# A gated mix of sliding-window attention and an MLP, one decode step: order and shape of the first and last transfers

## The chip, the cores and the metric

The kernel runs on one core of one Trainium2 chip. The metric is the device time of one launch in microseconds (us). The engines are named as in the profile: PE (TensorE matmul), PEld (its weight loads), DVE (VectorE), ACT (ScalarE), POOL (GpSimd) and SP (SyncE, which here only issues transfers). A "q" behind a name is the engine's sequencer. Sixteen DMA engines move the data.

## The reference

One token `x` of 576 elements goes through two branches, which a scalar gate mixes. All inputs are bf16.

```python
def reference(A_x, A_k_cache, A_v_cache, A_wq, A_wo, B_x, B_w1, B_b1, B_w2, B_b2, gate_w):
    x = A_x                                               # [1, 1, 576]
    g = sigmoid((x * gate_w).sum(-1, keepdims=True))
    # attention: 32 query heads, 16 KV heads of width 128, the last 4096 of 32768 keys
    q = (x @ A_wq).reshape(1, 1, 32, 128).transpose(0, 2, 1, 3)
    k = repeat(A_k_cache[:, :, -4096:, :], 2, axis=1)
    v = repeat(A_v_cache[:, :, -4096:, :], 2, axis=1)
    p = softmax(einsum("bhqd,bhkd->bhqk", q, k) * 128 ** -0.5)
    o = einsum("bhqk,bhkd->bhqd", p, v)
    a = o.transpose(0, 2, 1, 3).reshape(1, 1, 4096) @ A_wo
    # MLP: 576 -> 4608 -> 576
    h = gelu_tanh(x @ B_w1 + B_b1)
    b = h @ B_w2 + B_b2
    return g * a + (1 - g) * b                            # [1, 1, 576]
```

Keys and values are 16.8 MB each, the four weight matrices 4.7 or 5.3 MB each: some 53.6 MB are read once for an output of 1,152 bytes.

## The kernel before, in words

**Loads.** Nearly every load is issued by SP on one queue. A load of keys or values (`load_kv`, L102) brings two heads: for each head 64 partitions, each with one row of 16,384 bytes. The first 64 partitions of the tile are the first head, the others the second. Eight such loads bring the keys, eight the values, into a pool of six tiles, which w_2 shares at the end. The matrices w_q, w_1 and w_o go through a pool of three tiles; `load_flat` (L120) brings a slice of the matrix that is laid out flat over 128 partitions, so that each partition gets one contiguous row: 18,432 bytes for each of the two w_q tiles.

**Order of the issues.** The schedule is written by hand: the program text is the order on each engine. SP's order at the start is k_t[0] (L102), x9 (L136, x spread over 64 partitions, 9 elements each), the two w_q tiles (L120), k_t[1] and k_t[2] (L102), then the halves of b_1 (L557), w_1 and further keys and values. Three rows of 576 elements are issued by ACT instead: x_row (L130), gw_row (L131, the gate's weights) and b_2 into row 0 of b2_r (L132). POOL clears b2_r first (L129), so the load of b_2 waits for that clearing, while those of x_row and gw_row wait for nothing. The framework hands each transfer one of eight completion counters in turn; a transfer that gets a counter again waits for the counter's last user to have landed.

**Start of the computation.** PE first spreads x9 over the partitions (x_ps, L373), from which DVE makes the columns x2 (L381). DVE multiplies x_row and gw_row and sums them (L385), PE spreads the sum (g_ps, L390), and ACT and DVE make the gate g and omg = 1 - g of it (L392 to L397). Behind g_ps on PE stand the transposes of the first two heads' keys (L235), the product with w_q (q_ps, L409: 36 matmuls, of which the first four read the first 2,048 elements of the first tile), its turning (L421), and the first scores (L266).

**The middle.** For each head its keys are turned by PE (L235) and evicted by ACT and DVE (L246, L244). Scores (L266), softmax, and values (L342) follow behind. The two halves of w_1 are multiplied between the heads.

**The end.** The attention's output times w_o and the first three groups of w_2 are summed on PE in `part` (L671), with four rows of `part` on four column groups of the array at once. w_2 comes in four groups of nine rows per partition; the third is loaded in two pieces (rows 0 to 4, 5 to 8), the fourth in three (rows 0 to 5, 6 and 7, 8), all at L629. DVE adds (1 - g) times b_2 to `part` (part_s, L679). Then `row_matmul` (L690) sums the partitions of part_s and adds the nine rows of the last w_2 group into y_ps: output quarter t of 144 columns stands on partition 32 t. So the last four matmuls use row 8, one quarter each. DVE evicts all of y_ps with one instruction (L703), and SP writes the four partitions 0, 32, 64 and 96 of y to the output (L704).

In the profile trailing digits are left out of names: b_r is b2_r or b1_r, w_t is w1_t or w2_t, x is x9 or x2.

Of the kernel before, what the change touches and what calls it, by code (L numbers as in the profile page):

```python
# [9 lines left out]
BF16 = mybir.dt.bfloat16  # L10
# [6 lines left out]
def kernel(  # L17
# [15 lines left out]
    nc = tc.nc  # L33

    P = 128
    D = 576
# [10 lines left out]
    NQ = 4  # L47
    DQ = D // NQ

    RJ = 9  # L50
    NG = F // (P * RJ)


    NM = 9


    QC = Hq * Dh // 8
# [21 lines left out]
    const = ctx.enter_context(tc.tile_pool(name="const", bufs=1))  # L79
# [11 lines left out]
    wq_flat = A_wq.rearrange("a b -> (a b)").rearrange("(p n) -> p n", p=P)  # L91
    w1_flat = B_w1.rearrange("a b -> (a b)").rearrange("(p n) -> p n", p=P)
    w2_view = B_w2.rearrange("(g p j) n -> g p (j n)", p=P, j=RJ)
# [5 lines left out]
    def load_kv(cache, m, name):  # L99
        t = kv_pool.tile([P, NCK, Dh], BF16, name=name, tag="kv")  # L100

        nc.sync.dma_start(  # L102
            out=t[:],
            in_=cache[0, 2 * m : 2 * m + 2, Sk - W : Sk, :].rearrange(
                "e (p c) d -> p e (c d)", c=NCK
            ),
        )
        return t

    def load_k(m):  # L110
        return load_kv(A_k_cache, m, "k_t")
# [3 lines left out]

    WMAX = 41 * 256

    def load_flat(src, lo, n, name):
        t = w_pool.tile([P, WMAX], BF16, name=name, tag="w")
        nc.sync.dma_start(out=t[:, 0:n], in_=src[:, lo : lo + n])  # L120
        return t

    k_tiles, v_tiles = {}, {}

    x_row = const.tile([1, D], BF16, name="x_row")
    gw_row = const.tile([1, D], BF16, name="gw_row")

    b2_r = const.tile([P, D], BF16, name="b2_r")
    nc.gpsimd.memset(b2_r[:], 0.0)  # L129
    nc.scalar.dma_start(out=x_row[:], in_=A_x.rearrange("a b d -> (a b) d"))  # L130
    nc.scalar.dma_start(out=gw_row[:], in_=gate_w.rearrange("(o n) -> o n", o=1))  # L131
    nc.scalar.dma_start(out=b2_r[0:1, :], in_=B_b2.rearrange("(o n) -> o n", o=1))  # L132

    k_tiles[0] = load_k(0)
    x9 = const.tile([P // 2, NM], BF16, name="x9")
    nc.sync.dma_start(out=x9[:], in_=A_x.rearrange("a b (i m) -> (a b i) m", m=NM))  # L136
    wq_t = []
    QP = 2 * NM
    for i in range(2):
        wq_t.append(load_flat(wq_flat, i * QP * QC, QP * QC, "wq_t"))  # L140

    k_tiles[1] = load_k(1)

# [12 lines left out]
        out=row_f[:], in_=ident_f[:, 0 : 32 * (NQ - 1) + 1 : 32], axis=AX.X, op=ALU.add  # L156
# [4 lines left out]
        out=dup[:].rearrange("k (i e) -> k i e", e=2),  # L161
        in_=ident[0 : P // 2, 0 : P // 2].rearrange("k (i e) -> k i e", e=1).to_broadcast(
            [P // 2, P // 2, 2]
        ),
    )
    par = const.tile([P, 2], FP32, name="par")
    for o in range(2):
        nc.vector.tensor_reduce(
            out=par[:, o : o + 1],
            in_=ident_f[:].rearrange("p (i o) -> p o i", o=2)[:, o, :],  # L170
# [7 lines left out]
        out=turn[:].rearrange("p j (h q) -> p j h q", h=OJ),  # L178
        in_=ident[:].rearrange("p (o q j) -> p j o q", o=1, j=OJ).to_broadcast(
            [P, OJ, OJ, P // OJ]  # L180
        ),
# [4 lines left out]
        out=m_r[:], in_=ident_f[:].rearrange("p (s r) -> p r s", r=R), axis=AX.X, op=ALU.add  # L186
# [5 lines left out]
        out=row_e[:], in_=ident_f[:].rearrange("p (a e q) -> p e a q", e=2, q=2), axis=AX.XY,  # L192
# [3 lines left out]
        out=row_e[:], in0=row_e[:], scalar1=-MASK, scalar2=MASK, op0=ALU.mult, op1=ALU.add  # L196
    )
    mask = const.tile([P, BC * P], BF16, name="mask")
    for e in range(2):
        nc.vector.tensor_copy(  # L200
            out=mask[:, e::2], in_=row_e[:, e : e + 1].to_broadcast([P, BC * P // 2])
# [4 lines left out]
        out=m_c[:], in_=ident_f[:].rearrange("p (t c r) -> p c t r", c=BC, r=R), axis=AX.XY,  # L206
# [4 lines left out]
        out=m_hl[:], in_=ident_f[:].rearrange("p (h q) -> p h q", h=OJ), axis=AX.X, op=ALU.add  # L211
# [10 lines left out]
    for dst, src in ((sel, ident), (sel_f, ident_f)):  # L222
        nc.vector.tensor_copy(
            out=dst[:].rearrange("p l (o h) -> p l o h", o=2),
            in_=src[:].rearrange("p (h l x) -> p l x h", h=2, l=2)[:, :, 0:2, :],
# [149 lines left out]
    for dst, src, s in (  # L375
# [10 lines left out]
        out=junk[:], in0=x_row[:], in1=gw_row[:], scale=1.0, scalar=0.0,  # L386
# [11 lines left out]
        out=omg[:], in0=g_t[:], scalar1=-1.0, scalar2=1.0, op0=ALU.mult, op1=ALU.add  # L398
# [7 lines left out]
    for b in range(NM * NQ):  # L406
        m, t = b // NQ, b % NQ
# [22 lines left out]
    for m in range(HB // 2):  # L430
        lo = R * (NGR - 1) + RP * m
        nc.vector.tensor_copy(  # L432
            out=qz[:, m :: HB // 2, lo : lo + RP],
            in_=qT[:, :, m, :].rearrange("p i b -> p b i"),
# [7 lines left out]
    def w1_load(i):  # L442
        return load_flat(w1_flat, i * W1N, W1N, "w1_t")
# [105 lines left out]
    for h in range(NU):  # L549
# [4 lines left out]
        if h == 1:  # L554

            for o in range(2):
                nc.sync.dma_start(  # L557
                    out=b1_r[o : o + 32 * (NQ - 1) + 1 : 32],
                    in_=B_b1.rearrange("(o t k n) -> o t k n", o=2, t=NQ, k=2)[o],
# [57 lines left out]
    for i in range(NOG // 2):  # L617
        t = w_pool.tile([P, WMAX], BF16, name="wo_t", tag="w")
        nc.sync.dma_start(
            out=t[:, 0 : 2 * OJ * D].rearrange("p (o n) -> p o n", o=2),  # L620
            in_=wo_view[:, 2 * i : 2 * i + 2, :],
# [2 lines left out]
    w2_t = []  # L624
    for g in range(NG):
        t = kv_pool.tile([P, NCK * Dh], BF16, name="w2_t", tag="kv")
        cut = {NG - 2: (0, 5, RJ), NG - 1: (0, 6, 8, RJ)}.get(g, (0, RJ))
        for lo, hi in zip(cut, cut[1:]):
            nc.sync.dma_start(out=t[:, lo * D : hi * D], in_=w2_view[g, :, lo * D : hi * D])  # L629
        w2_t.append(t)  # L630

    ot = const.tile([P, Hq], BF16, name="ot")
# [1 line left out]
        out=ot[:], in0=o_sb[:], scalar=g_t[:, 0:1], in1=r_sums[:], op0=ALU.mult, op1=ALU.mult  # L634
# [3 lines left out]
    for j in range(OJ):  # L638
# [3 lines left out]
        out=ow_m[:],  # L642
# [5 lines left out]
    with nc.allow_low_precision("one of the eight summands is not zero"):  # L648
        nc.vector.tensor_reduce(  # L649
            out=ow[:].rearrange("p j o -> p (j o)"), in_=ow_m[:], axis=AX.X, op=ALU.add  # L650
# [4 lines left out]
    y_ps = ps_s.tile([P, DQ], FP32, name="y_ps", tag="s")  # L655
# [12 lines left out]
    for n, four in enumerate(blocks):  # L668
# [11 lines left out]
        out=part_s[:], in0=b2_r[:].rearrange("p (k n) -> p k n", k=2), scalar=omg[:, 0:1],  # L680
# [5 lines left out]
    quarters = [slice(t * DQ, (t + 1) * DQ) for t in range(NQ)]  # L686
# [10 lines left out]
    for j in range(RJ):  # L697
# [1 line left out]
        row_matmul(  # L699
            gt[:, j, NG - 1 : NG], [row[:, q] for q in quarters], False, j == RJ - 1  # L700
        )
    y = const.tile([P, DQ], BF16, name="y")
    nc.vector.tensor_copy(out=y[:], in_=y_ps[:])  # L703
    nc.sync.dma_start(  # L704
        out=out.rearrange("a b (t n) -> (a b t) n", t=NQ), in_=y[0 : 32 * (NQ - 1) + 1 : 32, :]
    )


# [28 lines left out]
```

## Time and profile before

| | before |
|---|---|
| time, median of 3 runs (all) | 134.98 us (134.93 to 135.19) |
| profiled execution: time | 134.92 us |
| profiled execution: span, first to last instruction | 133.0 us |
| busy PE / DVE / ACT / POOL | 90.9 / 61.3 / 48.5 / 4.2 us |
| read from memory | 53.62 MB, 403 GB/s over the span |
| first issue on SP (k_t[0]) and on ACT (x_row) | both at 0.73 us |
| POOL's clearing of b2_r | 0.73 us, 0.58 us long |
| x_ps on PE (needs x9) | 8.80 us |
| product of x_row and gw_row on DVE (L385) | 9.61 us |
| first transposes on PE | 10.98 us |
| last group of w_2: start of the first and the last matmul | 128.55 and 129.6 us |
| eviction of y_ps, issue of the result | 129.95 and 130.29 us |

The span counts from the first to the last instruction that the profiler saw; the time of an execution is longer by what lies around it. Windows give, for a stretch of the span, the busy time of each engine, the granted clock of TensorE as a share of its full speed, the mean busy share of the 16 DMA engines, and the rate at which bytes moved. In short windows the last two are rough: a packet's whole length and all of its bytes are booked where it starts.

### The profile page before, as it was taken

What the parts mean: (1) busy time and instruction counts of PE and PEld (TensorE: products, weight loads), DVE (VectorE), ACT (ScalarE), POOL (GpSimd) and SP (SyncE); (2) the same over time, 40 slices, a digit from 0 to 9 for tenths busy, and PEclk for the clock granted to TensorE, in tenths of its full rate; (3) what the DMA queues carried; (4) which work ended last, traced back from release to release, by engine and by line L of the source; (5) the groups of instructions that cost most, each with busy time, mean ns of one, the idle gap of its engine ahead of it and who ended that gap; (6) DMA issues with size and microseconds to landing.
All of it is one profiled execution on the core that took longest, in us unless ns stands there. A gap on an engine that the chain in (4) does not pass through costs nothing.

```text
span 133.0 us, 2659 instructions
## 1 busy us (share of the span) xinstructions
PE 90.9 (68%) x1127; PEld 58.6 (44%) x1127; DVE 61.3 (46%) x165; ACT 48.5 (36%) x91; POOL 4.2 (3%) x11
## 2 busy tenths in 40 slices
PE   0007985299296899969076996978988648459660
PEld 0007741267174565645045654645655215135340
DVE  4964632035227665575004257564866463440020
ACT  3003750066336787757001153766584100000000
POOL 8400000000000000000000000000000000000000
PEclk9999999757999999999955559999999955555865
DMA  3999999999999999999899999999999999999960
GB/s 79 400 430 432 443 424 429 434 436 412 431 458 399 453 414 446 409 421 479 379 453 409 448 414 443 419 439 424 434 429 429 415 418 430 436 424 415 428 261 0
DMA packets 4553, 53.79 MB, mean 404 GB/s; under 512 B 563, under 2 KB 702, under 8 KB 1214
## 3 DMA queue, kind: packets, MB, share of 16 engines
q1 hardware_dynamic: 4536, 53.62, 95.2%
q8 instruction: 9, 0.15, 0.4%
q14 instruction: 2, 0.02, 0.0%
q10 hardware_dynamic: 6, 0.00, 0.0%
HBM read 53.62 MB, written 0.00 MB: 403 GB/s over the span
## 4 chain that ended last, share of the span: by engine, by line
DMA 58%; PE 28%; DVE 8%; SPq 2%; issue 2%; DVEq 0%
DMA w_t<-in_B_w_dram 41%; DMA k_t<-in_A_k_cache_dram 17%; PE tp L235 13%; PE s_ps L266 4%; PE acc L342 3%; DVE kT L244 3%; PE h_ps L454 2%; PE hT L481 2%; DVE a_s L358 2%; PE y_ps L690 1%; SPq L120 1%; SPq L102 1%; DVE ez L320 1%; DVE part_s L679 1%; DVE h_r L472 1%
## 5 line engine op out<-in xcount | busy, mean ns | idle before, releaser
L246 ACT CAST kT<-tp 128x512 bf16<-128x512 f32 x80 | 44.1, 586 | 44.2 <-PE tp L235 43.7
L244 DVE CAST kT<-tp 128x512 bf16<-128x512 f32 x48 | 33.0, 690 | 38.6 <-PE tp L235 34.1
L235 PE MATMUL tp<-ident,k_t 128*128 128x128 bf16 x512 | 45.5, 238 | 4.7 <-DMA k_t<-in_A_k_cache_dram 3.0
L235 PEld LDWEIGHTS <-k_t 128*128 128x128 bf16 x512 | 35.2, 107 | 17.4 <-issue 12.8
L342 PE MATMUL acc<-v_t,ez 128*32 128x512 bf16 x128 | 13.3, 459 | 2.2 <-DVE a_s L358 1.9
L266 PE MATMUL s_ps<-kT,qz 128*32 128x512 bf16 x128 | 13.5, 416 | 0.3 <-DVE qz L432 0.3
L454 PE MATMUL h_ps<-w_t,x 128*32 128x288 bf16 x72 | 4.0, 365 | 6.8 <-DMA w_t<-in_B_w_dram 6.8
L454 PEld LDWEIGHTS <-x 128*32 128x32 bf16 x72 | 2.8, 117 | 7.6 <-issue 7.1
L373 PE MATMUL x_ps<-x,dup 64*128 64x9 bf16 x1 | 0.2, 163 | 8.8 <-DMA x<-in_A_x_dram 8.8
L342 PEld LDWEIGHTS <-ez 128*32 128x32 bf16 x128 | 3.7, 102 | 5.5 <-issue 3.1
L266 PEld LDWEIGHTS <-qz 128*32 128x32 bf16 x128 | 3.3, 94 | 3.8 <-issue 0.8
L679 DVE SCALAR_TENSOR_TENSOR part_s<-b_r,omg,part 128x576 f32<-128x576 bf16 x1 | 0.8, 814 | 8.8 <-PE part L671 8.8
L671 PE MATMUL part<-wo_t,ow 128*1 128x288 bf16 x64 | 4.0, 443 | 1.0 <-DVE ow L649 1.0
L671 PE MATMUL part<-w_t,gt 128*1 128x288 bf16 x54 | 3.7, 364 | 1.4 <-DMA w_t<-in_B_w_dram 1.4
L358 DVE SCALAR_TENSOR_TENSOR a_s<-acc,m_c,a_s 128x128 f32<-128x128 f32 x12 | 4.2, 351 | 0.4
L307 ACT ACTIVATE pr<-ms,nb 128x512 bf16<-128x512 f32 x4 | 2.9, 722 | 4.1 <-DVE nb L304 4.1
L320 DVE COPY ez<-pT 128x64 bf16<-128x64 bf16 x32 | 3.6, 183 | 1.7 <-PE pT L315 1.5
L148 DVE CAST ident_f<-ident 128x128 f32<-128x128 bf16 x1 | 3.0, 3000 | 1.8 <-POOL ident masks.py:199 1.8
L365 PE MATMUL o_ps<-m_r,a_s 128*128 128x8 f32 x8 | 1.9, 315 | 2.8 <-DVE a_s L358 2.8
L365 PEld LDWEIGHTS o_ps<-m_r,a_s 128*128 128x128 f32 x8 | 1.6, 249 | 4.9 <-DVE a_s L358 2.5
L671 PEld LDWEIGHTS <-gt 128*1 128x1 bf16 x54 | 2.2, 104 | 2.9 <-issue 2.0
L481 PE MATMUL hT<-sel_f,h_r 128*64 128x4 f32 x36 | 2.7, 264 | 1.2 <-DVE h_r L472 1.2
(82 smaller groups left out, 48.2 us busy)
## 6 DMA issues: line engine op xcount, KB each, us to landing
k_t<-in_A_k_cache_dram SPq DMA_DIRECT2D x8, 2048.0 KB, 27.5
v_t<-in_A_v_cache_dram SPq DMA_DIRECT2D x8, 2048.0 KB, 24.5
w_t<-in_B_w_dram SPq DMA_DIRECT2D x2, 2592.0 KB
wq_t<-in_A_wq_dram SPq DMA_DIRECT2D x2, 2304.0 KB, 14.4
wo_t<-in_A_wo_dram SPq DMA_DIRECT2D x2, 2304.0 KB
w_t<-in_B_w_dram SPq DMA_DIRECT2D x2, 1296.0 KB, 21.6
w_t<-in_B_w_dram SPq DMA_DIRECT2D x1, 864.0 KB
w_t<-in_B_w_dram SPq DMA_DIRECT2D x1, 720.0 KB, 21.3
```

The source lines that it names most:

```text
L148: nc.vector.tensor_copy(out=ident_f[:], in_=ident[:])
L235: nc.tensor.matmul(tp[:, c * P : (c + 1) * P], lhsT=k_tiles[h // 2][:, (h % 2) * NCH + i * BC + c, :], rhs=ident[:], start=True, stop=True,)
L244: nc.vector.tensor_copy(out=dst, in_=tp[:])
L246: nc.scalar.copy(out=dst, in_=tp[:])
L266: nc.tensor.matmul(s_tiles[b][32 * t : 32 * (t + 1), :], lhsT=qz[:, h // 2, lo : lo + 32], rhs=kT[h][:, i * BC * P : (i + 1) * BC * P], st ...
L320: nc.vector.tensor_copy(out=ez[:, b % 2, m, NQ * s : NQ * (s + 1), :, RP * m : RP * (m + 1)], in_=pT[:].rearrange("p c (t s r) -> p t c s ...
L342: nc.tensor.matmul(acc[b][32 * ct : 32 * ct + 4 * R, :, :], lhsT=ez[:, b % 2, ul // 2, n, :, :].rearrange("p c r -> p (c r)"), rhs=v_tiles ...
L358: nc.vector.scalar_tensor_tensor(out=a_s[:], in0=acc[b][:, c, :], scalar=m_c[:, c : c + 1], in1=a_s[:], op0=ALU.mult, op1=ALU.add,)
L365: nc.tensor.matmul(o_ps[:], lhsT=a_s[:], rhs=m_r[:], start=True, stop=True)
L454: nc.tensor.matmul(h_box[0][32 * t : 32 * (t + 1), k, 0:FB], lhsT=x2[:, m, :], rhs=w[:, off : off + FB], start=(m == 0), stop=(m == NM - 1),)
L481: nc.tensor.matmul(box[0][64 * e : 64 * (e + 1), j, :], lhsT=rows[:, j : j + RJ * 63 + 1 : RJ], rhs=sel_f[:, e, :], start=True, stop=True,)
L671: nc.tensor.matmul(part[32 * t : 32 * t + 1, k, 0:DB], lhsT=col, rhs=w[:, i * D + k * DB : i * D + (k + 1) * DB], start=(n == 0), stop=(n ...
```

## The change

Five places change.

1. `load_flat` can load its tile in pieces, and call a function between the first piece and the second. The first w_q tile is loaded in two: its first 2,048 elements per partition (128 rows of 4,096 bytes, 512 KB) are the first transfer of SP; then come k_t[0] and x9, and then the other 7,168 elements.
2. ACT's first transfers are now those of b_2, which wait for the clearing of b2_r; those of x_row and gw_row come behind them.
3. b_2 and x_row are loaded in halves of 288 elements each.
4. The last row of the last w_2 group is loaded in two pieces: its first 432 elements per partition, and its last 144, which only the last matmul reads.
5. y is a single row of 576 elements on one partition. The four quarters of y_ps are copied into it one by one, t = 0 and 1 by ACT, t = 2 and 3 by DVE. The result is written from one row instead of four.

```diff
-    def load_flat(src, lo, n, name):
+    def load_flat(src, lo, n, name, cuts=(), between=None):
         t = w_pool.tile([P, WMAX], BF16, name=name, tag="w")
-        nc.sync.dma_start(out=t[:, 0:n], in_=src[:, lo : lo + n])
+        edges = (0, *cuts, n)
+        for i, (a, b) in enumerate(zip(edges, edges[1:])):
+            if i == 1 and between is not None:
+                between()
+            nc.sync.dma_start(out=t[:, a:b], in_=src[:, lo + a : lo + b])
         return t
...
     nc.gpsimd.memset(b2_r[:], 0.0)
-    nc.scalar.dma_start(out=x_row[:], in_=A_x.rearrange("a b d -> (a b) d"))
+
+    for o in (slice(0, D // 2), slice(D // 2, D)):
+        nc.scalar.dma_start(out=b2_r[0:1, o], in_=B_b2.rearrange("(o n) -> o n", o=1)[:, o])
+    for o in (slice(0, D // 2), slice(D // 2, D)):
+        nc.scalar.dma_start(out=x_row[:, o], in_=A_x.rearrange("a b d -> (a b) d")[:, o])
     nc.scalar.dma_start(out=gw_row[:], in_=gate_w.rearrange("(o n) -> o n", o=1))
-    nc.scalar.dma_start(out=b2_r[0:1, :], in_=B_b2.rearrange("(o n) -> o n", o=1))
-
-    k_tiles[0] = load_k(0)
+
     x9 = const.tile([P // 2, NM], BF16, name="x9")
-    nc.sync.dma_start(out=x9[:], in_=A_x.rearrange("a b (i m) -> (a b i) m", m=NM))
-    wq_t = []
+
+    def first_keys():
+        k_tiles[0] = load_k(0)
+        nc.sync.dma_start(out=x9[:], in_=A_x.rearrange("a b (i m) -> (a b i) m", m=NM))
...
     QP = 2 * NM
-    for i in range(2):
-        wq_t.append(load_flat(wq_flat, i * QP * QC, QP * QC, "wq_t"))
+    wq_t = [
+        load_flat(wq_flat, 0, QP * QC, "wq_t", (NQ * QC,), first_keys),
+        load_flat(wq_flat, QP * QC, QP * QC, "wq_t"),
+    ]
...
-        cut = {NG - 2: (0, 5, RJ), NG - 1: (0, 6, 8, RJ)}.get(g, (0, RJ))
-        for lo, hi in zip(cut, cut[1:]):
-            nc.sync.dma_start(out=t[:, lo * D : hi * D], in_=w2_view[g, :, lo * D : hi * D])
+        cut = {NG - 2: (0, 5 * D), NG - 1: (0, 6 * D, 8 * D, RJ * D - DQ)}.get(g, (0,))
+        for lo, hi in zip(cut, (*cut[1:], RJ * D)):
+            nc.sync.dma_start(out=t[:, lo:hi], in_=w2_view[g, :, lo:hi])
...
-    y = const.tile([P, DQ], BF16, name="y")
-    nc.vector.tensor_copy(out=y[:], in_=y_ps[:])
-    nc.sync.dma_start(
-        out=out.rearrange("a b (t n) -> (a b t) n", t=NQ), in_=y[0 : 32 * (NQ - 1) + 1 : 32, :]
-    )
+
+    y = const.tile([1, D], BF16, name="y")
+    for t in range(NQ):
+        copy = nc.scalar.copy if t < 2 else nc.vector.tensor_copy
+        copy(out=y[:, quarters[t]], in_=y_ps[32 * t : 32 * t + 1, :])
+    nc.sync.dma_start(out=out.rearrange("a b n -> (a b) n"), in_=y[:])
```

## The prediction

> **What bounds the kernel now.** I read the slices and queue shares of the page first, then the chain that ended last, then short windows at both ends of the span, because the change touches only the ends.
>
> ```profile
> DMA  3999999999999999999899999999999999999960
> q1 hardware_dynamic: 4536, 53.62, 95.2%
> DMA 58%; PE 28%; DVE 8%; SPq 2%; issue 2%; DVEq 0%
> ```
>
> The transfers run from the first slice to the last but one at nine tenths or more, one queue (SP's) moves 53.62 MB, and the chain is mostly transfer. Windows of 20 us between 5 and 127 us show 423 to 433 GB/s at a DMA share of 0.99 to 1.01. So compute in the middle is cover, and the time is: when the stream starts, plus its bytes, plus what follows its end. An edit counts if it moves the start, lengthens the stream, or changes what comes behind it. Now the start, in windows (columns: busy us and count of PE, PEld, DVE, ACT, POOL; clock; DMA share; GB/s, bytes booked at a row's start):
>
> ```profile
> 1.60:1.70 0.10, 0.00 (x0) 0.00 (x0) 0.00 (x0) 0.00 (x0) 0.10 (x1) 1.00 0.04 12
> 2.10:2.30 0.20, 0.00 (x0) 0.00 (x0) 0.20 (x1) 0.20 (x1) 0.20 (x2) 1.00 3.62 655
> 2.30:2.70 0.40, 0.00 (x0) 0.00 (x0) 0.40 (x1) 0.40 (x1) 0.40 (x2) 1.00 0.00 0
> 2.70:2.95 0.25, 0.00 (x0) 0.00 (x0) 0.25 (x1) 0.25 (x1) 0.25 (x1) 1.00 1.45 524
> 2.95:3.50 0.55, 0.00 (x0) 0.00 (x0) 0.55 (x1) 0.31 (x1) 0.55 (x1) 1.00 0.00 0
> 3.50:3.90 0.40, 0.00 (x0) 0.00 (x0) 0.40 (x1) 0.00 (x0) 0.40 (x1) 1.00 1.73 655
> ```
>
> The reader is to see three things. x_row, from ACT, moves first (12 GB/s x 0.1 us, one row of 1,152 B). Then k_t[0] starts in two halves: 655 GB/s x 0.2 us and 524 x 0.25 are 131 KB each, eight rows of 16 KB, so eight of the 16 engines start near 2.2 and the other eight 0.6 later. The first eight rows are slow (3.62 x 0.2 x 16 / 8 = 1.45 us each; the second eight 1.45 x 0.25 x 16 / 8 = 0.73; the next sixteen 0.69). The second round begins at 3.5. Had the engines worked at the later 0.61 us a row, the stream would have begun near 2.9. The end, from the timeline:
>
> ```profile
> 126.50 0.54 PE L671 MATMUL part<-w_t,gt 128*1 128x288 bf16 x9 [0.90 <-DMA w_t<-in_B_w_dram]
> 127.08 0.81 DVE L679 SCALAR_TENSOR_TENSOR part_s<-b_r,omg,part 128x576 f32<-128x576 bf16 x1 [8.78 <-PE part L671]
> 127.95 0.66 PE L690 MATMUL y_ps<-part_s,row_f 128*1 128x144 f32 x8 [0.91 <-DVE part_s L679]
> 128.55 1.35 PE L690 MATMUL y_ps<-w_t,gt 128*1 128x144 bf16 x36
> 129.95 0.31 DVE L703 CAST y<-y_ps 128x144 bf16<-128x144 f32 x1 [2.06 <-PE y_ps L690]
> 130.29 0.60 SPq L704 DMA_DIRECT2D out_dram<-y  x1
> ```
>
> and in windows:
>
> ```profile
> 128.50:129.27 0.77, 0.77 (x32) 0.71 (x31) 0.00 (x0) 0.00 (x0) 0.00 (x0) 0.50 0.46 166
> 129.27:129.57 0.30, 0.30 (x16) 0.20 (x8) 0.00 (x0) 0.00 (x0) 0.00 (x0) 0.50 0.00 0
> 131.50:131.70 0.20, 0.00 (x0) 0.00 (x0) 0.00 (x0) 0.00 (x0) 0.00 (x0) 0.50 0.03 6
> ```
>
> The last byte of w_2 moves before 129.27, the last four matmuls start at 129.6 (the tile view of w_t), 0.34 later, though eight groups of four from 128.55 leave little slack: transfer and TensorE end within about 0.1 us of each other. Then one eviction of 0.31, the issue at 130.29, the result's rows 1.24 later, and 1.4 us of closing that the change leaves alone.
>
> **The change, part by part.** The sum goes against the profiled execution: 134.92 us, span 133.0, 1.9 outside it; the median of the runs is 0.06 above it.
>
> *Head: -0.45.* Two things. ACT's first transfer now waits for POOL's memset of b2_r, which ends at 1.31 (0.73 + 0.58), so SP's first transfer, still issued at 0.73, has nothing ahead. Its issue may shorten from the 0.66 of k_t[0] to the 0.54 of later lone k_t issues: -0.1. And the first transfer is one block of 128 rows of 4,096 B, not two heads of 64 rows of 16 KB. If all 16 engines start together, what is won lies between nothing (the first rows are slow for a reason common to all; the second round stays at 3.5) and the whole difference of a slow first row and the second eight's: all engines at 2.1 with rows as quick as 0.73 gives 2.85 for the first 16 KB in place of 3.5 to 3.8, so -0.8. With the -0.1, bounds 0 and -0.9. I take the middle: neither row decides, since no plain block starts an idle queue here.
>
> *Longer stream in front: +0.05.* w_q's first tile comes in 128 more rows and one more transfer, and ACT's three small transfers are five. Rows of 4.6 to 10 KB (105 to 127 us) run at 425 GB/s, rows of 16 to 20 KB at 427 to 433: up to 2% on 2.3 MB, 5.4 us, so 0 to 0.1.
>
> *Order and waits in front: 0.* k_t[0] lands 0.5 MB later, 512 KB / 430 GB/s = 1.2 us. gw_row, which was ACT's second transfer and is its fifth, lands later still: gw moved in the window 4.15:4.20 and b2 in 6.00:6.10, 1.9 us apart once 16 KB rows run beside them. Four steps behind a first at 2.3 to 4.2 give 10 to 12, a microsecond to see completion, so the gate product L385 (9.61 before) starts at 11 to 13, and the transposes behind g_ps on TensorE slip from 10.98 by 1.3 to 3. Behind them stand q_ps, q_r, qT and the first scores, then:
>
> ```profile
> 25.75 1.46 PE L235 MATMUL tp<-ident,k_t 128*128 128x128 bf16 x12 [3.00 <-DMA k_t<-in_A_k_cache_dram]
> SPq L557 <- DMA k_t<-in_A_k_cache_dram: 4.0, 1, 4.0
> ```
>
> That 3.0 us wait for k_t[1], whose place in the stream does not move, takes the slip. If that cover went, the next one is the queue: k and v loads land 22 to 32 us after issue, so transfers do not run dry. The second row is the other mechanism in front: a transfer that reuses one of eight completion counters waits for the counter's last user. With eleven transfers in the head instead of eight, w_q's second piece waits on SP until the first piece has landed (about 4 us), with w_q's second tile, k_t[1] and k_t[2] queued behind it, each waiting for a counter too (halves of b2, then k_t[0]). Meanwhile the 2 MB of k_t[0] are in the queue until about 8.3, so 4 us cover it; uncovered, the stream would idle for the excess.
>
> *Last row in two pieces: +0.06.* In 128.50:129.27, 0.46 x 0.77 x 16 = 5.7 us of engine time move 128 KB, 44 ns per KB against 37.5 in mid-run, about 8 ns a row beyond its bytes at 1,152 B. Eight more rows per engine are 0.06; the first three quarters are ready about 0.1 sooner, the fourth sets the end. Bounds 0 and +0.15 (a 288 B row as dear as half a 1,152 B one). The Trainium skill's page "DMA: Bandwidth & Descriptors" (Specifications) says that transfers below 512 B miss the line rate because of a read-modify-write. The four 288 B rows of the old result with their completions took 0.03 x 0.2 x 16 = 0.1 us in all, about 24 ns a row, so no penalty shows on that side; loads of 288 B into SBUF no row here shows. If that rule doubled the rows' time, the sum would be some 0.15 higher, an estimate from that page.
>
> *Four copies for one: +0.18.* DVE's eviction takes 309 ns for 144 columns; one partition costs as much, since columns set it (680 to 690 ns for 512). ACT: 586 ns for 512 columns, 171 for one, so 0.29 for 144. Each engine has two in line. Those for t = 0, 1, 2 can start about 0.1 sooner, t = 3 about 0.06 later, so the pairs end at 129.86 + 0.57 to 0.62 = 130.43 to 130.48 against 130.26. Overlap of neighbours (L246 x2: 1.07 for 2 x 0.586) takes off up to 0.1, a second engine to wait for adds up to 0.1: bounds +0.08 and +0.35.
>
> *Result as one row: -0.2.* 1.24 us lie between issue and the four 288 B rows; x_row, one row of 1,152 B, took 0.9 (0.73 to the window 1.60:1.70). Same shape: -0.34; same queue and direction as before: 0. Nearer in shape, so past the middle.
>
> **Sum:** -0.45 + 0.05 + 0 + 0.06 + 0.18 - 0.2 = -0.36 us: 134.92 becomes 134.56, the median 134.98 becomes 134.6.
>
> **Rivals.** *Nothing at the head.* The second round starts at 3.5 whatever comes first, for all sixteen first rows end together there, early or late starters. Against it: x_row moved at 1.6, so memory answers before. Then +0.05 + 0.06 + 0.18 - 0.2 = +0.09: 135.1. *The whole head.* All engines at full pace from 2.1, and x_row's latency for the result: -0.9 + 0.05 + 0.06 + 0.18 - 0.34 = -0.95: 134.0. For it: the second eight rows took 0.73. *The copies at the end (slower).* Two copies in line on each engine, ACT idle since 105 us, then SP waiting for both, behind a last quarter that lands late: +0.35 + 0.15 + 0.05, nothing back from the result's row, and a head of no more than -0.1: +0.45, 135.4. It decides from where the copies end 0.4 us later than 130.26 less what the head gave. For it: every copy price here is a bounded estimate upwards; against it: the last 0.3 us are the only serial work added.
>
> **Chances.** Forecast 0.50 (own range 134.3 to 134.8), whole head 0.12, nothing at the head 0.22, copies 0.16. 0.2% (0.27 us) is what a measurement tells from no change: below 134.7 is faster. Faster: 0.12 + 0.40 of the forecast; same: its other 0.10 + 0.20 of nothing at the head; slower: 0.16 + 0.02. The range 134.0 to 135.3 leaves out parts of the two outer cases.
>
> **What would show it.** Right: bytes from all engines at once near 2.0, the second round of rows before 3.3, the stream's end earlier by as much, DVE's last copy 0.1 to 0.3 behind its old distance from the last matmul, the result's row less than 1.24 after its issue. Wrong: the stream still at full rate only from 3.5; the last matmul over 0.5 us behind the last byte; a transfer gap near 4 or 8 us (the counters); a DMA share below 0.98 between 20 and 40 us (the slip not covered).

## The result, and the profile after

| | before | after |
|---|---|---|
| time, median of 6 runs each | 135.08 us (134.93 to 135.28) | 134.12 us (134.10 to 134.21) |
| ratio, 95% interval | | 0.9931 (0.9921 to 0.9941) |
| profiled execution: time / span | 134.92 / 133.0 us | 134.11 / 132.4 us |

The changed kernel is faster by 0.7%, 0.96 us. The forecast was 0.36 us, with a range of 134.0 to 135.3: the sign and this range held, but the size was less than half of what came, and 134.12 lies outside the forecast's own 134.3 to 134.8. The windows at the start, as before (busy us and count of PE, PEld, DVE, ACT, POOL; clock; DMA share; GB/s):

```profile
1.60:1.70 0.10, 0.00 (x0) 0.00 (x0) 0.00 (x0) 0.00 (x0) 0.10 (x1) 1.00 0.00 0
1.70:2.10 0.40, 0.00 (x0) 0.00 (x0) 0.26 (x1) 0.00 (x0) 0.40 (x2) 1.00 1.84 195
2.10:2.30 0.20, 0.00 (x0) 0.00 (x0) 0.20 (x1) 0.00 (x0) 0.20 (x2) 1.00 0.26 41
2.30:2.70 0.40, 0.00 (x0) 0.00 (x0) 0.40 (x1) 0.00 (x0) 0.40 (x2) 1.00 0.38 102
2.70:2.95 0.25, 0.00 (x0) 0.00 (x0) 0.25 (x1) 0.00 (x0) 0.25 (x1) 1.00 0.90 328
2.95:3.50 0.55, 0.00 (x0) 0.00 (x0) 0.55 (x1) 0.11 (x1) 0.55 (x1) 1.00 0.97 372
```

No x_row at 1.6 any more. Rows move from 1.7; the first are slow here too (1.84 x 0.4 x 16 = 11.8 us for 19 rows of 4 KB, 0.6 us each), but from 2.7 the stream runs near its pace, where before nothing began between 2.95 and 3.5. Over the first microseconds together, before and after:

```profile
1.00:5.00 4.00, 0.00 (x0) 0.00 (x0) 3.12 (x4) 1.28 (x1) 3.69 (x7) 1.00 0.72 246
```

```profile
1.00:5.00 4.00, 0.00 (x0) 0.00 (x0) 3.12 (x4) 1.28 (x1) 3.69 (x7) 1.00 0.87 291
```

45 GB/s more for 4 us are 0.18 MB, 0.4 us at 430 GB/s. The end, from the timeline of the changed kernel:

```profile
126.17 0.54 PE L684 MATMUL part<-w_t,gt 128*1 128x288 bf16 x9 [0.86 <-DMA w_t<-in_B_w_dram]
126.74 0.81 DVE L692 SCALAR_TENSOR_TENSOR part_s<-b_r,omg,part 128x576 f32<-128x576 bf16 x1 [9.48 <-PE part L684]
127.61 0.66 PE L703 MATMUL y_ps<-part_s,row_f 128*1 128x144 f32 x8 [0.91 <-DVE part_s L692]
...
128.22 1.48 PE L703 MATMUL y_ps<-w_t,gt 128*1 128x144 bf16 x36
...
129.57 0.56 ACT L719 CAST y<-y_ps 1x144 bf16<-1x144 f32 x2 [23.50 <-PE y_ps L703]
129.64 0.64 DVE L719 CAST y<-y_ps 1x144 bf16<-1x144 f32 x2 [2.08 <-PE y_ps L703]
130.34 0.27 SPq L720 DMA_DIRECT2D out_dram<-y  x1
```

The stream's landmark, the matmuls that wait for the last piece of w_2's third group, starts 0.33 earlier (126.17 against 126.50). The result is issued 0.05 *later* than before (130.34 against 130.29), so in this execution the split last row and the copies ate the head's gain. Executions differ here: two more profiles of the changed kernel have the issue at 130.06 and 130.16. But this issue takes 0.27 instead of 0.60, and the row moves in the window 131.05:131.20 instead of 131.50:131.70:

```profile
131.05:131.20 0.15, 0.00 (x0) 0.00 (x0) 0.00 (x0) 0.00 (x0) 0.00 (x0) 0.50 0.02 8
```

Then comes what was not forecast: the closing. After its last issue SP looks at ten semaphores, two to an instruction, before the engines' last barrier; the eight completion counters are among them. Before, then after (SP's semaphore instructions of the closing line: count; min/median/max ns; first and last start; then SP's wait there for the result's counter: us in total, times, longest):

```profile
L732 SPq EVENT_SEMAPHORE  x7: 17/28/28, 131.9 to 133.0; - x7
SPq L732 <- DMA out_dram<-y: 1.0, 1, 1.0
```

```profile
L746 SPq EVENT_SEMAPHORE  x7: 17/28/28, 130.7 to 132.3; - x7
SPq L746 <- DMA out_dram<-y: 0.6, 1, 0.6
```

Two of the seven belong to the barrier. Before, the result's counter was in the first of the other five: SP came to it at 131.942, after the landing, and then took four more, 0.065 apart, to 132.198. After, its counter is in the last: SP takes the four others from 130.675 on, while the row is on its way, and the fifth at 131.502 ends the wait. Which counter the result gets follows from how many transfers stand ahead of it, as they take the eight in turn. The change adds four: two pieces of w_q, two halves twice, two pieces of the last row. That moved it from the fourth counter to the eighth; SP's list does not run in the order in which the counters are handed out, and the fourth stands in its first pair, the eighth in its last.

### The profile page after: what moved, and what is told of

Same layout as the page of the kernel before. It is cut to its first block, busy times and chain, and to the rows that moved or that the text cites. A ratio compares the mean times of both kernels' runs of the same rounds, so it can differ in the third digit from the quotient of the medians.

```text
span 132.4 us, 2667 instructions
## 1 busy us (share of the span) xinstructions
PE 92.7 (70%) x1127; PEld 60.2 (45%) x1127; DVE 61.6 (47%) x166; ACT 49.3 (37%) x93; POOL 4.2 (3%) x11
## 4 chain that ended last, share of the span: by engine, by line
DMA 60%; PE 27%; DVE 7%; issue 2%; ACT 1%; SPq 1%; DVEq 0%; POOLq 0%; POOL 0%; ACTq 0%
DMA w_t<-in_B_w_dram 42%; DMA k_t<-in_A_k_cache_dram 15%; PE tp L248 12%; PE s_ps L279 4%; PE acc L355 4%; DMA b_r<-in_B_b_dram 3%; DVE kT L257 3%; PE hT L494 2%; DVE a_s L371 2%; PE y_ps L703 2%; PE h_ps L467 1%; ACT kT L259 1%; DVE part_s L692 1%; DVE h_r L485 1%; PE o_ps L378 0%
## 5 line engine op out<-in xcount | busy, mean ns | idle before, releaser
L248 PE MATMUL tp<-ident,k_t 128*128 128x128 bf16 x512 | 47.8, 247 | 3.7 <-DMA k_t<-in_A_k_cache_dram 2.2
L248 PEld LDWEIGHTS <-k_t 128*128 128x128 bf16 x512 | 37.4, 112 | 17.1 <-issue 13.5
L279 PE MATMUL s_ps<-kT,qz 128*32 128x512 bf16 x128 | 14.4, 442 | 0.3 <-DVE qz L445 0.3
L719 ACT CAST y<-y_ps 1x144 bf16<-1x144 f32 x2 | 0.5, 268 | 23.5 <-PE y_ps L703 23.5
L684 PE MATMUL part<-w_t,gt 128*1 128x288 bf16 x54 | 2.9, 285 | 3.1 <-DMA w_t<-in_B_w_dram 3.1
```

Source lines behind the costliest of these rows:

```text
L248: nc.tensor.matmul(tp[:, c * P : (c + 1) * P], lhsT=k_tiles[h // 2][:, (h % 2) * NCH + i * BC + c, :], rhs=ident[:], start=True, stop=True,)
L279: nc.tensor.matmul(s_tiles[b][32 * t : 32 * (t + 1), :], lhsT=qz[:, h // 2, lo : lo + 32], rhs=kT[h][:, i * BC * P : (i + 1) * BC * P], st ...
L684: nc.tensor.matmul(part[32 * t : 32 * t + 1, k, 0:DB], lhsT=col, rhs=w[:, i * D + k * DB : i * D + (k + 1) * DB], start=(n == 0), stop=(n ...
```

## The experiments

All ratios are to the kernel before, run on the same chip, with 95% intervals. The first four kernels shared one chip, the next four another, the last four the first chip again, later; the changed kernel stood beside the last eight.

**1. The counter alone.** The kernel before with four more transfers in its middle, and the changed kernel with the same four:

```diff
-                nc.sync.dma_start(out=b1_r[o : ... : 32], in_=B_b1...[o])
+                for k in range(2):
+                    nc.sync.dma_start(out=b1_r[o : ... : 32, k, :], in_=B_b1...[o][:, k, :])
...
-        nc.sync.dma_start(out=t[:, 0 : 2 * OJ * D]..., in_=wo_view[:, 2 * i : 2 * i + 2, :])
+        for o in range(2):
+            nc.sync.dma_start(out=t[:, o * OJ * D : (o + 1) * OJ * D], in_=wo_view[:, 2 * i + o, :])
```

> The kernel before, with four more transfers in its middle (each half of b_1 in two, each w_o tile in two, the same rows): the result's transfer then gets the last of the eight completion counters in SP's closing list instead of the first. Nothing else is touched. Theory (place of the counter): in the profile of before SP looked at the result's counter first and at four more pairs after it, 132.198 - 131.942 = 0.26 us behind the landing; with the counter last these four are looked at while the result is on its way, so the time falls by 0.26 us (134.98 to 134.7, ratio 0.998). Rival (the closing is set by something else, or the four looks cost nothing): no change, ratio 1.000; the four transfers themselves could add up to 0.05.

Measured: 134.77 against 135.10, ratio 0.9976 (0.9966 to 0.9985), 0.2 to 0.45 us faster. Its trace differs from that of before in nothing else at the end: the result is issued at 130.26, and

```profile
L739 SPq EVENT_SEMAPHORE  x7: 17/28/28, 130.9 to 132.7; - x7
```

SP starts looking at 130.9, 0.66 us before the result has landed (131.58), and the span ends at 132.735 instead of 133.017: 0.28. The counter's place is worth that, with the kernel's two ends as they were.

> The changed kernel with the same four more transfers: the result's counter is the first in SP's closing list again, all else as changed. Theory (place of the counter): 0.26 us slower than the changed kernel, 134.12 to 134.4 (ratio to before 0.995). Rival (the shorter closing comes from the single row or from what else changed): as the changed kernel, 134.1 (0.993).

Measured: 134.97, ratio 0.9990 (0.9968 to 1.0012), with runs from 134.5 to over 136. The direction agrees, but the interval holds neither the theory's 0.995 nor the rival's 0.993, and the size can't be read: in its profiled execution (135.77) one of the sixteen DMA engines still brought its rows of the last three pieces until 130.09, alone for the last microsecond, when the others had ended by 129.1. Why this variant's stream spread so is open. Its closing went as the theory says: first look 132.586, 0.35 after the landing at 132.239, last 132.842, 0.26 later.

**2. The end alone.** The kernel before with the four copies and the single row (the diff's last part), nothing else.

> The kernel before with the changed end alone: four copies onto one partition, result written as one row; its counter stays first in the closing list. Theory (a single row starts sooner): the flight from issue to landing is 0.80 instead of 1.31 us (-0.51), the copies with the wait for two engines cost +0.26, so -0.25: 134.7 (ratio 0.998). Rival 1 (the row's short flight came with the idle queue or the other counter, not with the single row): flight near 1.3, +0.26, 135.2 (1.002). Rival 2 (the copies cost nothing since they overlap the last matmul): -0.5, 134.5 (0.996).

Measured: 134.84 against 135.10, ratio 0.9979 (0.9971 to 0.9988), 0.26 us. The last of its matmuls starts at 130.007, then:

```profile
130.31 0.56 ACT L705 CAST y<-y_ps 1x144 bf16<-1x144 f32 x2 [22.98 <-PE y_ps L690]
130.38 0.64 DVE L705 CAST y<-y_ps 1x144 bf16<-1x144 f32 x2 [2.10 <-PE y_ps L690]
131.08 0.28 SPq L706 DMA_DIRECT2D out_dram<-y  x1
```

```profile
131.75:131.95 0.20, 0.00 (x0) 0.00 (x0) 0.00 (x0) 0.00 (x0) 0.00 (x0) 0.50 0.02 6
```

From the last matmuls' start to the issue 1.08 us, against 0.68 before: the copies cost 0.4 where all quarters are ready together. From the issue to the landing (131.88) 0.80, against 1.31: the single row gives back 0.51, with the counter still first, so it is the row and not the counter. Rivals 1 and 2 fall.

**3. The head, part by part.** k_t[0] first again; ACT's transfers in the old order; both in the changed kernel with the result's counter kept last.

```diff
+    first_keys()
     wq_t = [
-        load_flat(wq_flat, 0, QP * QC, "wq_t", (NQ * QC,), first_keys),
+        load_flat(wq_flat, 0, QP * QC, "wq_t"),
```

> The changed kernel with k_t[0] and x9 first again and w_q's first tile in one piece behind them; one w_o tile in two, so that the result's counter stays last. ACT's transfers still wait for the memset. Theory (the plain block starts all engines at once): the first 16 KB rows start in two halves again, the stream ends 0.25 to 0.33 us later, 134.12 to 134.4 (ratio 0.995). Rival (what counts is only that nothing of ACT's is ahead of SP's first transfer): at most 0.1 slower, 134.15 (0.993 to 0.994).

Measured: 134.58, ratio 0.9966 (0.9954 to 0.9979). The changed kernel gave 0.9931, 0.9926 and 0.9934 in its three sets, so having the block of w_q in front is worth about 0.35%, 0.5 us, more than the rival allows. Its head, with ACT still behind the memset:

```profile
1.70:2.10 0.40, 0.00 (x0) 0.00 (x0) 0.25 (x1) 0.00 (x0) 0.40 (x2) 1.00 0.00 0
2.10:2.30 0.20, 0.00 (x0) 0.00 (x0) 0.20 (x1) 0.00 (x0) 0.20 (x2) 1.00 3.79 655
2.30:2.70 0.40, 0.00 (x0) 0.00 (x0) 0.37 (x4) 0.00 (x0) 0.40 (x2) 1.00 0.75 164
2.70:2.95 0.25, 0.00 (x0) 0.00 (x0) 0.25 (x3) 0.00 (x0) 0.25 (x1) 1.00 0.65 262
2.95:3.50 0.55, 0.00 (x0) 0.00 (x0) 0.55 (x4) 0.08 (x1) 0.55 (x1) 1.00 0.18 60
```

Nothing before 2.1, eight rows at 2.1 to 2.3, four more before 2.7 and four after: nearly the picture of before, although no transfer of ACT's was ahead.

```diff
-    for o in (slice(0, D // 2), slice(D // 2, D)):
-        nc.scalar.dma_start(out=b2_r[0:1, o], ...)
     for o in (slice(0, D // 2), slice(D // 2, D)):
         nc.scalar.dma_start(out=x_row[:, o], ...)
     nc.scalar.dma_start(out=gw_row[:], ...)
+    for o in (slice(0, D // 2), slice(D // 2, D)):
+        nc.scalar.dma_start(out=b2_r[0:1, o], ...)
```

> The changed kernel with ACT's five small transfers in the old order: x_row's halves and gw_row first, waiting for nothing, b_2's halves last behind the memset. Their number is the same, so the result's counter stays last. Theory (SP's first transfer starts sooner when none of ACT's is ahead of it: 1.77 instead of 2.17 us): the stream starts and ends 0.1 to 0.4 us later, 134.12 to 134.2 to 134.5 (ratio to before 0.994 to 0.996). Rival (the block alone makes the early start): as the changed kernel, 0.993; the gate's product would start sooner than 10.5, and nobody would notice.

Measured: 134.12 beside 134.03 for the changed kernel, ratios 0.9946 (0.9925 to 0.9967) and 0.9926 (0.9915 to 0.9938): no difference that these runs tell. The head decides, and for the rival:

```profile
1.70:2.10 0.40, 0.00 (x0) 0.00 (x0) 0.26 (x1) 0.00 (x0) 0.40 (x2) 1.00 1.85 196
```

196 GB/s from 1.7, as with the memset (195). Putting ACT behind the memset does nothing for the start. (The ratio alone does not decide: its interval holds the theory's 0.994 to 0.996 and the rival's 0.993.)

**4. Plain, or short?** The first block is plain and its rows are short. One piece of 18,432 B rows tells these apart, and so do keys with short rows:

```diff
-        load_flat(wq_flat, 0, QP * QC, "wq_t", (NQ * QC,), first_keys),
+    wq_t = [load_flat(wq_flat, 0, QP * QC, "wq_t")]
+    first_keys()
```

> The changed kernel with w_q's first tile as first transfer in one piece, 128 rows of 18,432 bytes instead of 4,096, then k_t[0] and x9 (one w_o tile in two, so the result's counter stays last). Theory 1 (all engines start at once because the block is plain, not two heads): the first rows start near 1.75 on all engines as now, the stream keeps its gain, 0.993 to 0.994; x9 lands some 4 us later and the wait for k_t[1] may not cover it, without effect on the stream. Theory 2 (the rows must be short, so that the engines have several on the way): the first rows are slow again, about 1.4 us each, 0.3 to 0.5 us of the head are lost, 0.996.

Measured: 134.01, ratio 0.9923 (0.9910 to 0.9937), beside 134.20, 0.9934 (0.9920 to 0.9948), for the changed kernel: as good at least, and the try that came nearest to a better version, though the intervals overlap. In 1.7 to 2.1 us

```profile
1.70:2.10 0.40, 0.00 (x0) 0.00 (x0) 0.25 (x1) 0.00 (x0) 0.40 (x2) 1.00 2.71 553
1.00:5.00 4.00, 0.00 (x0) 0.00 (x0) 3.12 (x4) 1.28 (x1) 3.70 (x7) 1.00 0.84 290
```

twelve rows of 18 KB start (553 x 0.4 = 221 KB), each slow (1.4 us), and the first 4 us still come to 290 GB/s. So the rows need not be short. That it is the plain block which counts, and not w_q in place of the keys, is not separated: every run here with a plain block first loads w_q first, and every run with two blocks first loads keys. x9 comes late here (x_ps at 13.9) and costs nothing.

```diff
+        k0 = A_k_cache[0, 0:2, Sk - W : Sk, :].rearrange("e (p c) d -> p e (c d)", c=NCK)
+        for a, b in ((0, NQ * QC), (NQ * QC, NCK * Dh)):
+            nc.sync.dma_start(out=k_tiles[0][:, a // Dh : b // Dh, :], in_=k0[:, :, a:b])
```

> The changed kernel with k_t[0] as first transfer in two pieces, its first 4,096 bytes per partition ahead, then the rest, x9 and w_q whole; as many transfers as in the changed kernel. So short rows, but two heads of 64 rows. Theory 1 (the plain block matters): eight engines start near 2.2 and the others at 2.4 to 2.8, as with k_t[0] whole, and the time is 0.4 us above the changed kernel, 0.996. Theory 2 (short rows matter): as the changed kernel, 0.993.

Measured: 135.65, ratio 1.0032 (1.0019 to 1.0045), 1.5 us above the changed kernel and so worse than either theory. Two losses:

```profile
2.10:2.30 0.20, 0.00 (x0) 0.00 (x0) 0.20 (x1) 0.00 (x0) 0.20 (x2) 1.00 0.16 41
2.30:2.70 0.40, 0.00 (x0) 0.00 (x0) 0.40 (x1) 0.00 (x0) 0.40 (x2) 1.00 0.79 174
1.00:5.00 4.00, 0.00 (x0) 0.00 (x0) 3.12 (x4) 1.28 (x1) 3.70 (x7) 1.00 0.66 202
...
8.00:9.00 1.00, 0.00 (x0) 0.00 (x0) 0.14 (x2) 0.00 (x0) 0.00 (x0) 1.00 0.67 242
```

A head of 202 GB/s, 0.8 us behind the changed kernel's (two transfers of two heads in a row), and a dip near 8.5 us, about 0.4 us; the last 0.3 us are not placed. That nothing moves before 2.1 speaks against theory 2. But theory 1's two halves do not show: two rows start by 2.3 (41 x 0.2 = 8 KB) and seventeen by 2.7 (174 x 0.4 = 70 KB). The cause of the dip is open.

**5. The rest of the change.** The last row in one piece (`8 * D, RJ * D - DQ` back to `8 * D`); b_2 and x_row whole; a first piece of 2,048 B rows (`(2 * QC,)`), a try at a better version. The first two keep the result's counter by splitting w_o loads.

> The changed kernel with the last row of w_2 in one piece (one w_o tile in two keeps the counter). Theory (as in the sum: eight more small rows per engine cost 0.08 us of stream, and t = 0 to 2 are ready 0.16 us before t = 3): the last bytes move 0.08 sooner, but all four quarters are ready together, later by 0.07 than the first three now, and DVE copies two in line from there: the end is the same within 0.1 us, ratio 0.993. Rival 1 (the early quarters carry the gain): 0.15 us slower, 0.994. Rival 2 (small rows are dear): 0.15 faster, 0.992.

Measured: 134.07, ratio 0.9936 (0.9923 to 0.9949), beside 134.03: the same within what these runs tell, some 0.2 us. The split pays for itself and no more.

> The changed kernel with b_2 and x_row whole again, and both w_o tiles in two so that the result's counter stays last. Theory (the halves do nothing but move the counter): as the changed kernel, 0.993. Rival (the halves matter by themselves, by rows or waits in the head): 0.1 us or more away from it.

Measured: 134.15, ratio 0.9938 (0.9926 to 0.9950), beside 134.03: 0.12 more, which is where the rival begins, but the two intervals overlap. That the halves do more than move the counter is not shown.

> The changed kernel with a first piece of w_q half as long: 128 rows of 2,048 bytes, 256 KB. A try at a better version. Theory 1: the start is set by the pattern, as the changed kernel, 0.993. Theory 2 (shorter rows hide more of the first latency): up to 0.2 us faster, 0.992. Against both: if the first piece moves out before the descriptors of k_t[0] are there, the engines pause and some of the head is lost, 0.994 to 0.995.

Measured: 134.60, ratio 0.9973 (0.9952 to 0.9995), spread from 134.17 to 135.97: worse. 262 GB/s over the first 4 us for 291, 0.3 us less. The packets of the trace agree with the warning in the expectation: near 3.0, 3.2 and 3.4 us only 9, 7 and 10 of the 16 engines have a row under way, where in the changed kernel all 16 have. A first piece of 256 KB does not keep the engines busy until k_t[0] is there.

The changed kernel itself, beside the variants of 3 and 5, and of 4:

> The changed kernel unaltered, beside the variants below on their chip, so that these can be read against it. Nothing to tell apart: 0.993 of before expected, with a spread of 0.1 us as in its first six runs.

> The changed kernel unaltered, once more beside the variants of the first transfer on their chip. 0.993 of before.

Measured: 134.03, ratio 0.9926 (0.9915 to 0.9938), and 134.20, ratio 0.9934 (0.9920 to 0.9948).

Together: the changed end alone is worth 0.26 us, the counter alone 0.33 and the block in front about 0.5. They add up to 1.1, against 0.96 for the whole change; each is known to some 0.15 us.

## Why the prediction was right in sign and short in size

| step | forecast | measured in the profiles |
|---|---|---|
| head with the longer stream | -0.40 | -0.33 (126.50 to 126.17); two more profiles of the changed kernel have 125.97 and 126.01 |
| order and waits in front | 0 | 0 |
| last row in two pieces | +0.06 | +0.14 (landmark to last matmul 3.25 for 3.11) |
| copies | +0.18 | +0.25 (last matmul to issue 0.92 for 0.68) |
| result as one row | -0.20 | -0.51 (issue to landing 0.80 for 1.31) |
| closing | 0 | -0.24 (landing to SP's last look 0.36 for 0.60) |
| sum | -0.36 | -0.69 of -0.81; the other 0.1 lies behind SP's last look (what is outside the span fell from 1.9 to 1.7), where no view shows its cause |

*Head.* The size was right, half of the reason was wrong. With the block of w_q in front the stream starts sooner (experiments 3 and 4, with the tensor not separated from the shape); that ACT's transfer was ahead of SP's first one cost nothing. The -0.33 is one pair of executions: the landmark is at 126.49 in `before_count` and 126.89 in `before_row`, which start as before, so experiment 3's 0.5 us is the better measure. Of the 0.4 us by which the first row comes sooner, 0.25 are a shorter issue (0.41 for 0.66). The issue's end to the first row took 0.63 us for the plain block (1.14 to 1.77) and, in the kernel before, 0.78 and 1.40 for the two heads (1.39 to 2.17 and 2.79). The Trainium skill's page "DMA: Bandwidth & Descriptors" (Specifications) gives about 0.6 us to the first byte on this path. Counted from the issue's end the plain block agrees, the two heads do not, and the page makes no such distinction. Why half of the engines start later with two heads was not tried.

*Order and waits in front.* Right that nothing is lost, though the slip was smaller than forecast. w_q's second piece was issued at 4.57, after the first had landed, with k_t[0] still in the queue; the first transposes slipped to 11.88, by 0.9 instead of 1.3 to 3, and the wait for k_t[1] fell from 3.00 to 2.23.

*Last row.* Mis-sized by 0.08, though within its bounds, and hidden in the next step: with the row whole the copies start later, and the time is the same (experiment 5). Rows of 288 B follow each other on an engine 0.015 us apart at the end of the changed trace, rows of 1,152 B 0.047 in that of `after_rows`: four of the small rows take 0.06 for the same bytes, a third more, so no doubling below 512 B shows on loads either.

*Copies.* 0.25, and 0.4 without the split of the last row. ACT and DVE take some 270 and 305 ns each, close to the estimate; what was missed is DVE's start 0.1 after its matmul's end instead of 0.05, and SP's issue 0.06 behind the copies instead of 0.03.

*Result as one row.* This is the term that was mis-sized most, beyond its own bounds of 0 and -0.34. The right row was at hand (x_row's 0.9), but 0.14 was held back because it was a load. A single row flew faster still: 0.75 from issue to moving, for the four rows' 1.24. Experiment 2 shows the same -0.51 with only the end changed.

*Closing.* This is the step that failed: "1.4 us of closing that the change leaves alone" was put at nothing and was worth -0.24 here, 0.33 in experiment 1. The four added transfers moved the result's counter from the first place of SP's closing list to the last. That the framework hands out counters in turn was used for the waits in front, and not followed to the end of the program.

The rival with the copies had their price nearly right (0.25 to 0.4 late), but behind them the single row and the closing gave back 0.75.

That 134.12 lies inside the wide range is in part luck. It lies close to the 134.0 of the rival "the whole head", whose head of -0.9 did not come: a head of about the forecast's size and an unforeseen closing stand in its place.

## What to carry to other kernels

Where the transfers bound a kernel, look at when *all* engines move their first rows, and try a plain block of 128 rows ahead of loads made of several blocks; here it was worth 0.5 us, with w_q as the block. Write a small result as one row from one partition: here it paid for its copies and 0.26 us more. And follow the last transfer's completion counter to the closing: it should be the one looked at last, and one harmless transfer more or less moves it.

## What the runs showed of the hardware that was not expected

- A store of four rows of 288 B took 0.60 us to issue and 1.31 to land; one row of 1,152 B 0.27 and 0.80.
- Each further look at a pair of semaphores costs SP some 0.065 us, serial, behind the landing (131.942 to 132.198 for four).
- A first transfer of two heads of 64 rows of keys (16 KB each) started eight rows at 2.1 to 2.3 us and eight more 0.2 to 0.6 us later. One of 128 rows of w_q started 0.4 sooner (1.77 for 2.17), with 19 rows of 4 KB or twelve of 18 KB begun by 2.1.
- The kernel whose first piece was a short piece of keys had a dip to 242 GB/s between 8 and 9 us that the changed kernel has not (431). Its cause was not tried.
